# Clustered attention and a multiplicative feed-forward on one core: routing two heads ahead, engine copies for heads 0 and 1, halved weight loads

## The chip, the cores and the metric

The kernel runs on one core of one Trainium2 chip. The metric is the time on the device in microseconds (us); a kernel's time is the median of several executions. Kernels are compared only within the same rounds.

## The reference, cut to what matters

Each of 4 x 8 = 32 heads (768 tokens of width 64) is attention in which a query sees only the keys that fall into the same one of 16 clusters. The result, 3072 tokens of width 512, goes through a feed-forward network (FFN).

```python
q_assign = argmax(einsum('bhsd,hcd->bhsc', q_n, c_n), -1)      # c_n: normalised centroids of the head
k_assign = argmax(einsum('bhsd,hcd->bhsc', k_n, c_n), -1)
scores = where(q_assign[..., :, None] == k_assign[..., None, :], q @ k^T / 8, -1e9)
attn_out = softmax(scores) @ v
# ... (rearranged to x: [3072, 512])
out = ((x @ w1) * (x @ w2)) @ w3 @ w_out
```

## The kernel before: the parts that matter

The program is a row of periods. Period p computes the scores and exponentials of head p and the attention products of head p-1, prepares later heads, and fills TensorE's gaps with FFN work. Until period 8 this fill is the product w3 @ w_out ("fold": 8 items of transposes pt, then 16 items of products pw); the FFN proper (pu, then po) follows from period 9. Items are sorted by a number between 0 and 1, their place within the period, and every engine runs its own instructions in that order.

A head goes through these steps: three loads (q, k, v); POOL splits q and k into a bfloat16 part and its rest (stg); stg is turned into xqk, by TensorE for the first ten heads and by a DMA transpose for the others; TensorE multiplies xqk by the centroids (route, into prr); VectorE reduces that to one-hot rows (rsc, mx, oh); TensorE turns these (route_turn, into pso); VectorE scales them (ohT); four small DMAs put them below the head's q and k in xqk. There they work as a mask: equal clusters cancel an offset of -256 in the scores.

```python
def prep(g):
    ...                                          # cut
    eng = nc.vector if g < 1 else nc.gpsimd
    for lo, hi in ((0, NCH), (NCH, NC2)) if g < 1 else ((0, NC2),):
        eng.tensor_copy(out=stg[:, lo:hi, 0:D], in_=qk32[:, lo:hi])
        eng.tensor_tensor(out=stg[:, lo:hi, D:P], in0=qk32[:, lo:hi],
                          in1=stg[:, lo:hi, 0:D], op=ALU.subtract)
    nc.gpsimd.tensor_copy(out=vb[:, :, 0:D], in_=x32[:, 2])

def turn_dma(g):                                 # heads 10 and later
    st["xqk"] = xtp.tile([P, NC2, P], BF16, name="xqk")
    nc.sync.dma_start_transpose(out=st["xqk"], in_=st.pop("stg"))

# route_turn(g), its end:
    nc.vector.tensor_scalar(out=ohT, in0=pso, scalar1=msc[:, 0:1], scalar2=msc[:, 1:2],
                            op0=ALU.mult, op1=ALU.add)
    for a in range(4):
        nc.sync.dma_start(xqk[D : D + C, 3 * a : 3 * a + 3, :], ohT[32 * a : 32 * a + C])

def in_period(p):                                # p from -3
    for g in LOADS.get(p, []): load(g)
    if PE_HEADS <= p + 3 < NG: turn_dma(p + 3)
    ...                                          # prep of head p+3 (p+4 from head 10 on), one or two weight loads
    work += [((i + 0.5) / 9, it) for i, it in enumerate(score_items(p))]
    work += [(0.50, turn_pe(p + 2, 0)), (0.62, turn_pe(p + 2, 1))]      # below head 10
    work += [(0.02, route(p + 1)), (0.36, route_turn(p + 1))]
    work += [(0.23 + 0.13 * i, it) for i, it in enumerate(av_items(p - 1))]
    ...                                          # join at 0.93, fold or FFN items
```

A head's one-hot rows are asked for at 0.36 of the period before it is scored, 0.7 of a period before its first score.

The softmax here doesn't subtract the row's maximum and nothing guards it: scores larger than these inputs give would overflow.

## Time and profile before

| Kernel before | |
|---|---|
| time, median of 4 runs | 326.12 us (323.71 to 327.62) |
| span of the profiled run, which was a slow one (330.3 us) | 328.5 us |
| TensorE busy | 284.7 us, 87% |
| first score matmul, first exponential | 26.5 us, 27.1 us |
| TensorE's waits for one-hot rows | 14.6 us |

Engines are PE (TensorE; PEld is its weight load), DVE (VectorE), ACT (ScalarE), POOL and SP. L with a number is a line of the kernel; the changed kernel has other numbers for the same statements. The first view is the page of the kernel before: span, busy time per engine, and three rows of tenths over 40 equal slices of the span (TensorE busy, TensorE's granted clock, DMA engines busy).

```profile
span 328.5 us, 7415 instructions
...
PE 284.7 (87%) x2896; PEld 176.2 (54%) x2938; DVE 164.1 (50%) x340; ACT 195.4 (59%) x351; POOL 99.8 (30%) x110
...
PE   0357799699878999997899998999999999899995
...
PEclk9995699879997999997999999999999999999999
DMA  6973969922466586776765557655532012001103
```

TensorE is the busiest engine. It is idle for more than half of the first four slices (33 us), and its clock row has dips. The next view is who waited for whom on TensorE: us in total, number of waits, the longest.

```profile
engine line waited for: us in total, times, longest us
PE sc L341 <- DMA xqk<-ohT: 14.6, 8, 4.0
...
PE prr L293 <- DVE xT_all L406: 4.4, 8, 0.8
```

The scores wait for the one-hot rows eight times, 14.6 us together. Next, the table by stretches of the kernel before: bounds and length in us, then busy time with the number of instructions per engine, granted clock, DMA share and GB/s.

```profile
core 0: us, PE busy (x) PEld busy (x) DVE busy (x) ACT busy (x) POOL busy (x), PEclk, DMA share, GB/s
28.00:32.00 4.00, 4.00 (x31) 3.17 (x30) 2.21 (x4) 1.97 (x5) 3.56 (x4) 0.51 0.08 12
36.00:40.00 4.00, 4.00 (x42) 3.17 (x40) 1.17 (x2) 1.68 (x3) 0.21 (x1) 0.50 0.95 232
160.00:180.00 20.00, 19.77 (x221) 12.29 (x224) 11.16 (x25) 15.44 (x29) 6.36 (x7) 1.00 0.76 156
```

From 160 to 180 us TensorE is busy for 19.77 of 20 us at full clock; only less work for TensorE would help there. The two early stretches lie just behind a wait of 4.0 and 2.0 us: TensorE is busy throughout, but at half its clock. Busy time times (1 - clock), summed over stretches of 4 us, is 11.8 us in this profile. Last, the start in the timeline of the kernel before: start in us, duration, engine, line, what it does; in brackets the idle time of the engine and what ended it.

```profile
12.00 0.17 DVE L158 COPY cnsrc<-cnsrc 128x64 bf16<-128x64 bf16 x1
12.07 1.63 POOL L265 TENSOR_TENSOR stg<-x_196,stg 128x768 bf16<-128x768 f32 x1
12.11 1.63 DVE L157 COPY cnsrc<-cnsrc 128x64 bf16<-128x64 bf16 x1
...
20.60 2.49 SPq L324 DMA_DIRECT2D xqk<-ohT  x4
...
26.50 1.03 PE L341 MATMUL sc<-xqk 80*128 80x512 bf16 x2 [3.96 <-DMA xqk<-ohT]
...
27.14 1.09 ACT L345 ACTIVATE ex<-sc 128x512 bf16<-128x512 f32 x2 [20.90 <-PE sc L341]
```

The same copy of 64 columns takes 0.17 us, and 1.63 us when POOL's subtraction runs beside it. This is what the Trainium skill, "SBUF — State Buffer" (Who interferes with whom), describes: VectorE and POOL hold a port pair in turn, and the second one blocks. The rows of head 0 are sent at 20.6 us and the first score starts at 26.5 us. The waits of score matmuls for the rows are therefore one cost, the low clock behind them a second, and the long start a third.

### The profile page before, as it was taken

How to read it: one execution, taken by the hardware profiler on the slowest of the kernel's cores; microseconds unless marked ns; L12 is line 12 of the kernel's file. 1: busy time of each engine (PE TensorE's matmuls, PEld its weight loads, DVE VectorE, ACT ScalarE, POOL GpSimd, SP SyncE). 2: the span in 40 equal slices, each digit the busy share in tenths (PEclk: the TensorE clock that was granted, in tenths of full speed). 3: DMA queues.
4: the chain of work that ended last, by engine and by line, in shares of the span. 5: the costliest groups of instructions: out<-in, count | busy, mean ns of one | idle time of the engine just before them, and what ended most of it. 6: DMA issues, size and time to landing. Idle time of an engine off the chain costs nothing.

```text
span 328.5 us, 7415 instructions
## 1 busy us (share of the span) xinstructions
PE 284.7 (87%) x2896; PEld 176.2 (54%) x2938; DVE 164.1 (50%) x340; ACT 195.4 (59%) x351; POOL 99.8 (30%) x110
## 2 busy tenths in 40 slices
PE   0357799699878999997899998999999999899995
PEld 0245566366655566654566564656565655444442
DVE  8883456347663555544546444545454543332431
ACT  3004466447685987875687776787777777332330
POOL 3745138334355543433343233333300000000000
PEclk9995699879997999997999999999999999999999
DMA  6973969922466586776765557655532012001103
GB/s 221 198 128 97 190 133 245 243 72 85 117 155 132 142 165 155 144 189 190 140 146 126 129 168 185 155 127 128 150 87 57 8 38 89 17 0 70 59 2 128
DMA packets 59283, 41.16 MB, mean 125 GB/s; under 512 B 38768, under 2 KB 54128, under 8 KB 59248
## 3 DMA queue, kind: packets, MB, share of 16 engines
q1 hardware_dynamic: 56016, 35.44, 42.0%
q0 software_dynamic: 3232, 5.24, 9.6%
q8 instruction: 23, 0.38, 0.5%
q14 instruction: 12, 0.10, 0.1%
HBM read 29.39 MB, written 6.29 MB: 109 GB/s over the span
## 4 chain that ended last, share of the span: by engine, by line
PE 77%; DMA 11%; DVE 5%; ACT 4%; issue 1%; SPq 0%; POOL 0%; DVEq 0%
PE pu L216 24%; PE sc L341 13%; PE po L235 12%; PE av L373 11%; DMA xqk<-ohT 9%; PE sc L351 5%; PE pw L191 3%; DMA w3b<-in_moe_w_dram 2%; PE prr L293 2%; PE pso L316 2%; ACT ex L345 2%; PE pst L283 2%; PE psx L405 1%; PE pt L178 1%; DVE xT_all L406 1%
## 5 line engine op out<-in xcount | busy, mean ns | idle before, releaser
L345 ACT ACTIVATE ex<-sc 128x512 bf16<-128x512 f32 x192 | 110.6, 599 | 61.2 <-PE sc L341 60.8
L341 PE MATMUL sc<-xqk 80*128 80x512 bf16 x192 | 70.5, 397 | 15.5 <-DMA xqk<-ohT 14.6
L355 ACT ACTIVATE ex<-sc 128x512 bf16<-128x512 f32 x96 | 57.7, 601 | 23.3 <-PE sc L351 23.2
L373 PEld LDWEIGHTS <-ex 128*128 128x128 bf16 x1152 | 49.6, 101 | 13.2 <-issue 2.2
L224 DVE TENSOR_TENSOR ab<-pu,asb 128x512 bf16<-128x512 f32 x48 | 33.2, 691 | 43.2 <-PE pu L216 38.5
L216 PE MATMUL pu<-xT_all,w1b 128*128 128x512 bf16 x177 | 47.7, 383 | 1.1 <-issue 0.2
L216 PE MATMUL pu<-xT_all,w2b 128*128 128x512 bf16 x182 | 47.3, 378 | 0.5
L235 PE MATMUL po<-wc,ab 128*128 128x512 bf16 x183 | 45.8, 382 | 0.5
L222 ACT CAST asb<-pu 128x512 bf16<-128x512 f32 x48 | 28.2, 587 | 27.9 <-PE pu L216 27.9
L351 PE MATMUL sc<-xqk 80*128 80x256 bf16 x192 | 38.3, 281 | 0.1
L320 DVE TENSOR_SCALAR ohT<-pso,msc 128x384 bf16<-128x384 bf16 x32 | 15.2, 474 | 27.8 <-PE pso L316 25.0
L235 PEld LDWEIGHTS <-ab 128*128 128x128 bf16 x192 | 18.6, 97 | 18.5 <-issue 0.2
L216 PEld LDWEIGHTS <-w1b 128*128 128x128 bf16 x192 | 18.6, 98 | 18.3 <-issue 0.6
L216 PEld LDWEIGHTS <-w2b 128*128 128x128 bf16 x192 | 18.4, 97 | 18.2 <-issue 0.3
L341 PEld LDWEIGHTS <-xqk 80*128 80x128 bf16 x192 | 17.3, 99 | 20.1 <-DMA xqk<-ohT 16.1
L351 PEld LDWEIGHTS <-xqk 80*128 80x128 bf16 x192 | 17.5, 101 | 15.4 <-issue 2.8
L297 DVE TENSOR_REDUCE rsc<-prr 128x192 f32<-128x384 f32 x32 | 17.7, 554 | 15.8 <-PE prr L293 15.8
L293 PEld LDWEIGHTS <-xqk 128*128 128x128 bf16 x384 | 14.3, 96 | 9.5 <-issue 5.8
L243 DVE COPY osb<-po 128x512 f32<-128x512 f32 x12 | 8.3, 692 | 21.0 <-PE po L235 19.0
L293 PE MATMUL prr<-cnt_181,xqk 128*128 128x32 bf16 x384 | 14.8, 177 | 4.6 <-DVE xT_all L406 4.4
L386 DVE TENSOR_TENSOR xtm<-av,rcp 128x384 bf16<-128x384 f32 x32 | 17.8, 557 | 1.1
L191 PE MATMUL pw<-wob,w3T 128*128 128x512 bf16 x56 | 16.0, 401 | 0.4
(170 smaller groups left out, 316.8 us busy)
## 6 DMA issues: line engine op xcount, KB each, us to landing
out_dram<-osb SPq DMA_DIRECT2D x24, 256.0 KB, 2.0
w3b<-in_moe_w_dram POOLq DMA_DIRECT2D x4, 512.0 KB, 7.7
xqk<-ohT SPq DMA_DIRECT2D x128, 12.0 KB, 1.8
wob<-in_moe_w_out_dram POOLq DMA_DIRECT2D x2, 512.0 KB, 7.0
w1b<-in_moe_w_dram POOLq DMA_DIRECT2D x2, 512.0 KB, 7.2
w2b<-in_moe_w_dram POOLq DMA_DIRECT2D x2, 512.0 KB, 10.0
xqk<-stg SPq DMA_TRANSPOSE x22, 4.5
x_105<-in_q_dram SPq DMA_DIRECT2D x1, 192.0 KB, 2.4
```

Of the source, the lines that this page charges most:

```text
L191: nc.tensor.matmul(st[jc], lhsT=w3T[:, kc, jc * P : (jc + 1) * P], rhs=wob[:, kc], start=(kc == 0), stop=(kc == 7),)
L216: nc.tensor.matmul(pu, lhsT=wb[:, fc, jc * P : (jc + 1) * P], rhs=xT_all[:, fc, t0 : t0 + TB], start=(fc == 0), stop=(fc == 3),)
L222: nc.scalar.copy(out=st["a"], in_=pu)
L224: nc.vector.tensor_tensor(out=st["ab"][:, jc], in0=pu, in1=st.pop("a"), op=ALU.mult)
L235: nc.tensor.matmul(st["o"], lhsT=st["ab"][:, jc, sub * P : (sub + 1) * P], rhs=wc[:, jc], start=(jc == 0), stop=(jc == 7),)
L293: nc.tensor.matmul(prr[:, j], lhsT=st["xqk"][:, j, :], rhs=cnt2[:, g % H], start=True, stop=True)
L341: nc.tensor.matmul(sc, lhsT=xqk[0:KR, NCH + 2 * pr + part, :], rhs=xqk[0:KR, 0:4, :], start=True, stop=True,)
L345: nc.scalar.activation(out=ex[:, part, 0:512], in_=sc, func=ACT.Exp, scale=SM_SCALE)
L351: nc.tensor.matmul(sc[:, i], lhsT=xqk[0:KR, NCH + 2 * pr + i, :], rhs=xqk[0:KR, 4:6, :], start=True, stop=True,)
L355: nc.scalar.activation(out=ex[:, :, 512:S], in_=sc, func=ACT.Exp, scale=SM_SCALE)
L373: nc.tensor.matmul(st["av"][:, sub, 0:VCOL], lhsT=st["exs"][j // 2][:, j % 2, sub * P : (sub + 1) * P], rhs=st["vb"][:, j, 0:VCOL], start= ...
L386: nc.vector.tensor_tensor(out=xtm_cur[0][:, :, (h % 2) * D : (h % 2) * D + D], in0=av[:, :, 0:D], in1=rcp.unsqueeze(2).to_broadcast([P, NC ...
```

## The change

Its intent: route two heads ahead, so that the one-hot rows are in place early; take POOL out of the way of the first two heads; place their rows by engine copies and not by DMA; load the weights in 20 pieces and not 10, two a period. The core of the diff, with cuts marked and some lines joined:

```diff
+FIRST = 2
+DIRECT = 2
+    for i in range(8):
+        wloads.append((w3b[:, i], w3v[:, i]))      # 20 loads in place of 10; w_out, w1, w2 alike (cut)
 def prep(g):
+        if g < FIRST:                                # per half, q or k; v on POOL as before (cut)
+                    nc.scalar.copy(out=stg[:, half, 0:D], in_=x32[:, i])
+                    nc.vector.tensor_tensor(out=stg[:, half, D:P], in0=x32[:, i],
+                                            in1=stg[:, half, 0:D], op=ALU.subtract)
 # route_turn(g)
+            if g < DIRECT:
+                for a in (2, 0, 3, 1):
+                    dst, src = xqk[D : D + C, 3 * a : 3 * a + 3, :], pso[32 * a : 32 * a + C]
+                    if a < 2: nc.scalar.copy(out=dst, in_=src)
+                    else:     nc.vector.tensor_scalar(out=dst, in0=src, scalar1=MASKB,
+                                                      scalar2=-MASKB, op0=ALU.mult, op1=ALU.add)
+                return
 # in_period(p)
-            work += [(0.50, turn_pe(p + 2, 0)), (0.62, turn_pe(p + 2, 1))]
-            work += [(0.02, route(p + 1)), (0.36, route_turn(p + 1))]
+            work += [(0.03, turn_pe(p + 2, 0)), (0.13, turn_pe(p + 2, 1))]
+        if p == 0: work += [(0.02, route_turn(1))]
+            work += [(0.33, route(p + 2)), (0.67, route_turn(p + 2))]
-        wload()                                      # one a period, two from period 2
+        wload(); wload()
```

Periods -3 to -1 become one hand-ordered stretch, begin(): loads of head 0 on two queues, centroid norm, heads 0 and 1 prepared and turned, route(0), route_turn(0), route(1), with head 2's preparation among them. The fold items are spread anew (1, 2, 2, 2, 1, 1, then 5 a period). The centroid chain has fewer small operations.

## The prediction

> **What bounds the kernel now.** TensorE: 284.7 of 328.5 us busy (busy table, 87%), against ACT 59%, DVE 50%; from 160 to 280 us the busy-by-stretch table has it at 97%. Three losses:
>
> 1. The start. The timeline has the first score matmul at 26.5 us. VectorE's centroid chain takes 5.95 to 13.74 us: most ops take 0.15 us, but four take 0.96 to 1.63 us while POOL prepares head 1. The Trainium skill, "SBUF — State Buffer" (Who interferes with whom), says a VectorE op with two SBUF inputs or in a 2-port mode blocks against a GpSimd op; the trace agrees (the same 64-column copy: 0.17 and 1.63 us).
> 2. Waits of scores for one-hot rows (xqk<-ohT): 14.6 us of TensorE in the table of waits, 4.0 of them at the start; 8.8% of the chain. Routing products wait 4.4 us more for the xT_all copy.
> 3. The clock: 0.51 at 28-32 us, 0.50 at 36-40 and 64-68, 0.57 at 100-104, 0.65 at 152-156, each after a wait of 2 to 4 us. "TensorE: Matmul & The Clock Gate" (Part 1) says an idle window of about 3.4 us halves it; the trace roughly agrees. Busy time times (1 - clock) sums to about 11 us.
>
> **What the change does.** TensorE work stays about 273 us at full clock (busy times clock, summed).
>
> - Start: head 0's q and k land near 4 us on two queues; ScalarE casts, VectorE subtracts, POOL keeps away. I estimate the centroid chain ends near 10 us, first routing product near 12, head 1's one-hots (serial: one PSUM buffer) near 17.5, first score 18.5, first exponential 20 (behind a 1.28 us table load) instead of 27.1. About 8 us earlier, but four fold transposes that filled this time (3.5 us) come later: net 5.
> - One-hots are issued over a period (6 to 8 us) ahead; issue to landing is 1.8 us in the median, 6.1 at worst. The other 10.6 us of waits nearly vanish, with about 8 of 11 us of clock loss. Routing at 0.33 instead of behind the join saves about 3 of 4.4 us.
> - Weight loads: same bytes, twice the issues (about 0.75 us of POOL each), spread to period 8. The first 85 us must now carry about 66 us of DMA that had 100. I estimate 4 us of new waits.
>
> **Critical path.** All lies there up to the pure FFN tail at 283 us. The first FFN product (period 9) should start near 83 to 88 us instead of 101.
>
> Sum: 325.9 - 5 - 10 - 8 - 3 + 4 = 304; I say 305 for imperfect packing.
>
> **Predicted: 305 us**, 8 in 10 between 297 and 313. Faster by over 2%: 0.96; within 2%: 0.03; slower: 0.01.
>
> **What shows it right.** First score at 17 to 20 us, first exponential near 20; TensorE's waits for xqk<-ohT under 2 us; clock near 1.0 after about 25 us (mean 0.98 or more); first pu matmul before 90 us; TensorE at 92% or more; still 45 us from last exponential to end.
>
> **What would make it wrong.** Periods 0 to 8 bound by DMA or POOL (pst waiting for stg, fold transposes for w3b); VectorE's routing chain ending after TensorE wants the one-hot transpose, a third of a period later; ScalarE holding the start, as head 1's row copies stand ahead of the first exponential; a clock left low by the sparse first 20 us.

## More of the kernel before

Executions of one kernel spread by up to three per cent here. One that took over 1.5% more than the fastest of its kernel is called slow; medians count all executions, ratios the fast ones alone.

A DMA transpose asked for at the start of period p is read by the routing product at 0.02 of period p+2: a lead of 2.02 periods.

## The result, and the profile after

| | before | after |
|---|---|---|
| time, median of 4 runs | 326.12 us | 313.62 us (313.19 to 315.29) |
| ratio | | 0.963 (95% interval 0.956 to 0.970) |
| span of the profiled run | 328.5 us | 313.4 us |
| first score, first exponential | 26.5, 27.1 us | 19.5, 22.2 us |
| TensorE's waits for one-hot rows (xqk<-ohT) | 14.6 us | none in the table |
| TensorE's waits for DMA transposes (xqk<-stg) | none | 8.8 us |
| busy time times (1 - clock), by the clock record | 11.8 us | 2.6 us |
| first FFN product (pu) | 101.8 us | 90.6 us |

A ratio is the mean time of one kernel's fast runs over that of the kernel before's fast runs of the same rounds, so it is not quite the ratio of the medians. The kernel is 3.7% faster. The prediction was 305 us with a range to 313 us: right in direction, too low in size, by 8.6 us.

The page of the changed kernel, in the same rows:

```profile
span 313.4 us, 7404 instructions
...
PE 279.5 (89%) x2899; PEld 170.9 (55%) x2938; DVE 156.4 (50%) x335; ACT 201.9 (64%) x363; POOL 101.4 (32%) x118
...
PE   1459997997599899979999999999999998999995
...
PEclk9999999999799999999999999999999999899999
DMA  6865569989916966587666686656732011002003
```

TensorE is mostly busy in slices 4 to 10 and its clock record is nearly whole, but slice 11 (78 to 86 us) is half empty. Up to about 27 us the record can't be trusted: it reads 1.00, while matmuls take the time of half a clock (last section). The waits of TensorE in the changed kernel (us in total, times, longest):

```profile
PE prr L317 <- DMA xqk<-stg: 8.8, 5, 5.5
...
PE pso L340 <- DVE oh_114 L325: 2.9, 2, 1.4
PE pso L340 <- DVE oh_113 L325: 1.9, 2, 1.0
...
PE pst L303 <- POOL stg L286: 0.5, 1, 0.5
```

The rows are no longer waited for. In their place stand routing products that wait for a DMA transpose. The table by stretches of the changed kernel, columns as before, around the largest of these waits (the DMA share is summed from the times of packets and can pass 1):

```profile
76.00:80.00 4.00, 0.73 (x15) 0.45 (x13) 0.64 (x1) 1.19 (x2) 0.00 (x0) 1.00 1.10 102
80.00:84.00 4.00, 1.81 (x16) 0.91 (x17) 1.20 (x3) 0.00 (x0) 0.00 (x0) 0.72 1.19 229
84.00:88.00 4.00, 3.94 (x40) 2.46 (x40) 1.90 (x5) 2.06 (x4) 2.92 (x3) 0.85 0.48 109
```

TensorE works 0.73 us of the 4 from 76 to 80, and the idle time is followed by a clock of 0.72 and 0.85. "TensorE: Matmul & The Clock Gate" (Part 1) says about 3.4 us of idleness are enough; the trace agrees with this wait of 5.46 us, and the clock record shows no other loss before 264 us. It is not the least that is enough: in the kernel before, low clock also came behind single waits of 2.04 us (36 us), 1.84 us (150 us) and 0.94 us (100 us). The timeline of the changed kernel there, SPq being the queue on SP that issues DMAs:

```profile
68.33 5.74 SPq L294 DMA_TRANSPOSE xqk<-stg  x1
...
82.19 0.50 PE L317 MATMUL prr<-cnt_110,xqk 128*128 128x32 bf16 x12 [5.46 <-DMA xqk<-stg]
```

The first DMA transpose (head 10) is asked for at 68.33 us. Its issue alone holds the queue for 5.74 us; the other 21 transposes of this profile took 1.3 to 2.3 us there. The routing product that reads it starts at 82.19 us. The list of DMA issues between 68 and 70 us (size in KB, us from issue to landing):

```profile
w2b<-in_moe_w_dram POOLq DMA_DIRECT2D x1, 256.0 KB, 8.4
w1b<-in_moe_w_dram POOLq DMA_DIRECT2D x1, 256.0 KB, 11.1
...
xqk<-stg SPq DMA_TRANSPOSE x1, 13.8
```

The transpose lands after 13.8 us, while two weight loads around it take 8.4 and 11.1 us. The median of all 22 transposes of this profile is 4.5 us. The start in the timeline of the changed kernel:

```profile
9.62 0.34 PE L317 MATMUL prr<-cnt_110,xqk 128*128 128x32 bf16 x6 [0.52 <-ACT xqk L306]
...
10.01 2.43 DVE L279 TENSOR_TENSOR stg<-x_129,stg 128x384 bf16<-128x384 f32 x2 [1.38 <-ACT stg L278]
...
12.11 1.82 POOL L286 TENSOR_TENSOR stg<-x_152,stg 128x768 bf16<-128x768 f32 x1
12.36 0.55 DVE L321 TENSOR_REDUCE rsc<-prr 128x192 f32<-128x384 f32 x1
...
14.75 0.35 DVE L350 TENSOR_SCALAR xqk<-pso 16x384 bf16<-16x384 bf16 x1 [0.60 <-PE pso L340]
...
15.20 0.47 ACT L348 COPY xqk<-pso 16x384 bf16<-16x384 bf16 x1 [1.04 <-DVE xqk L350]
...
16.09 0.47 ACT L348 COPY xqk<-pso 16x384 bf16<-16x384 bf16 x1 [0.43 <-DVE xqk L350]
...
19.46 0.63 PE L377 MATMUL sc<-xqk 80*128 80x512 bf16 x1
...
20.89 1.28 ACT L381 ACT_TABLE_LOAD   x1
...
22.19 1.08 ACT L381 ACTIVATE ex<-sc 128x512 bf16<-128x512 f32 x2
...
27.79 0.38 PE L377 MATMUL sc<-xqk 80*128 80x512 bf16 x1
```

Three things stand here. Head 0's routing product ends near 10 us, but VectorE's reduction of it (L321) starts only at 12.36 us, because two subtractions for head 1, at 0.55 us each when alone, take 2.43 us beside POOL. The row copies of head 0 follow one another, VectorE, ScalarE, VectorE, ScalarE, 14.75 to 16.56 us. And the table load of the exponential (1.28 us) stands behind the copies of head 1; that these would stand ahead of the first exponential is a risk that the prediction named. Besides, a score matmul of 512 columns takes 0.63 us at 19.46 and 0.38 us at 27.79.

### The profile page after: what moved, and what is told of

Same layout as the page of the kernel before. It is cut to its first block, busy times and chain, and to the rows that moved or that the text cites. A ratio compares the mean times of both kernels' runs of the same rounds, so it can differ in the third digit from the quotient of the medians.

```text
span 313.4 us, 7404 instructions
## 1 busy us (share of the span) xinstructions
PE 279.5 (89%) x2899; PEld 170.9 (55%) x2938; DVE 156.4 (50%) x335; ACT 201.9 (64%) x363; POOL 101.4 (32%) x118
## 3 DMA queue, kind: packets, MB, share of 16 engines
q0 software_dynamic: 3392, 5.24, 11.8%
## 4 chain that ended last, share of the span: by engine, by line
PE 69%; DMA 15%; DVE 5%; SPq 3%; ACT 3%; issue 2%; POOL 1%; POOLq 0%; DVEq 0%; ACTq 0%
PE pu L225 23%; DMA xqk<-stg 12%; PE po L244 12%; PE sc L377 10%; PE av L409 8%; PE sc L387 5%; PE pw L200 3%; SPq L79 3%; PE prr L317 3%; DMA x_543<-in_k_dram 2%; PE pso L340 2%; PE pst L303 2%; PE psx L441 2%; ACT ex L381 1%; DVE rsc L321 1%
## 5 line engine op out<-in xcount | busy, mean ns | idle before, releaser
L377 PE MATMUL sc<-xqk 80*128 80x512 bf16 x192 | 71.8, 388 | 1.8 <-ACT ex L381 1.1
L409 PEld LDWEIGHTS <-ex 128*128 128x128 bf16 x1152 | 47.5, 98 | 15.8 <-issue 0.8
L244 PE MATMUL po<-wc,ab 128*128 128x512 bf16 x182 | 44.8, 378 | 0.5
L321 DVE TENSOR_REDUCE rsc<-prr 128x192 f32<-128x384 f32 x32 | 17.8, 557 | 40.7 <-PE prr L317 40.7
L387 PE MATMUL sc<-xqk 80*128 80x256 bf16 x192 | 37.4, 276 | 0.1
L387 PEld LDWEIGHTS <-xqk 80*128 80x128 bf16 x192 | 16.8, 99 | 13.8 <-issue 2.2
L317 PEld LDWEIGHTS <-xqk 128*128 128x128 bf16 x384 | 13.8, 97 | 14.7 <-DMA xqk<-stg 11.1
L356 DVE TENSOR_SCALAR ohT<-pso,msc 128x384 bf16<-128x384 bf16 x30 | 14.2, 473 | 8.9 <-PE pso L340 8.2
L303 PE MATMUL pst<-ident,stg 128*128 128x128 bf16 x120 | 12.2, 250 | 7.1 <-DVE stg L279 6.7
```

Source lines behind the costliest of these rows:

```text
L244: nc.tensor.matmul(st["o"], lhsT=st["ab"][:, jc, sub * P : (sub + 1) * P], rhs=wc[:, jc], start=(jc == 0), stop=(jc == 7),)
L303: nc.tensor.transpose(out=pst[:, j], in_=st["stg"][:, half * NCH + j], identity=ident)
L317: nc.tensor.matmul(prr[:, j], lhsT=st["xqk"][:, j, :], rhs=cnt2[:, g % H], start=True, stop=True)
L321: nc.vector.tensor_reduce(out=rsc, in_=prr, axis=AX.X, op=ALU.add)
L377: nc.tensor.matmul(sc, lhsT=xqk[0:KR, NCH + 2 * pr + part, :], rhs=xqk[0:KR, 0:4, :], start=True, stop=True,)
L387: nc.tensor.matmul(sc[:, i], lhsT=xqk[0:KR, NCH + 2 * pr + i, :], rhs=xqk[0:KR, 4:6, :], start=True, stop=True,)
```

## The experiments

Each run was timed beside the kernel before. Runs of one group shared a chip. The expectation is quoted. Kernels of one group are compared by their fast runs. Group 1 has no run of the changed kernel itself.

| Group | Kernel | median us | mean of the fast runs, us (their number) | ratio to before (95%) |
|---|---|---|---|---|
| 1 | w_early | 307.65 | 305.0 (2) | 0.940 (0.927 to 0.952) |
| 1 | pe12 | 309.01 | 309.3 (4) | 0.953 (0.943 to 0.963) |
| 1 | lead | 303.11 | 302.4 (3) | 0.931 (0.918 to 0.945) |
| 1 | start | 307.69 | 307.0 (3) | 0.946 (0.936 to 0.956) |
| 2 | after_again | 309.76 | 308.2 (4) | 0.948 (0.941 to 0.956) |
| 2 | route1 | 321.20 | 320.7 (3) | 0.992 (0.984 to 1.000) |
| 2 | nodirect | 310.16 | 308.7 (4) | 0.950 (0.943 to 0.956) |
| 2 | best | 304.47 | 304.2 (4) | 0.936 (0.929 to 0.942) |
| 3 | after_3 | 311.27 | 309.1 (4) | 0.947 (0.940 to 0.955) |
| 3 | lead_2 | 306.40 | 306.1 (5) | 0.938 (0.933 to 0.943) |
| 3 | lead_nd | 306.06 | 305.6 (4) | 0.936 (0.931 to 0.942) |
| 3 | bigw | 311.31 | 310.3 (5) | 0.951 (0.944 to 0.957) |
| 4 | after_4 | 310.51 | 310.1 (4) | 0.950 (0.943 to 0.957) |
| 4 | early0 | 303.15 | 302.1 (4) | 0.926 (0.919 to 0.932) |
| 4 | lead_late | 308.61 | 308.1 (5) | 0.944 (0.939 to 0.949) |
| 5 | lead_3 | 304.66 | 304.5 (5) | 0.939 (0.934 to 0.945) |
| 5 | early0_2 | 302.20 | 302.2 (6) | 0.932 (0.928 to 0.936) |
| 5 | early0_few (wrong) | 299.35 | 299.3 (6) | 0.924 (0.919 to 0.928) |

Theory A was: the weight loads, which now reach period 8, collide with the first DMA transposes. The rival B: the transposes are asked for too late. turn_dma stayed at the start of period p, but its reader moved from 0.02 of period p+2 to 0.33 of period p+1, so the lead shrank from 2.02 to 1.33 periods.

### w_early: weight loads over sooner

```diff
-        wload()
-        wload()
+        wload(); wload(); wload()
```

> The changed kernel with three weight loads a period instead of two, so that they are all issued by period 5 and not period 8; nothing else. Theory A (the weight loads that now reach period 8 collide with the first DMA transposes and that costs the missing time): the first transpose lands in under 6 us instead of 13.8 us, the 5.5 us wait of TensorE for xqk<-stg at 77 to 82 us goes, and the time falls by 5 to 6 us, to about 308 us; the waits of 1 to 2 us after 90 us stay. Rival B (the transposes are only asked for too late, 1.33 periods before their use): the long wait mostly stays, time within 2 us of 313.6.

The first transpose landed in 4.4 us in place of 13.8 us (7.7 to 11.6 us in the three repeats below), and the first wait went: A holds for it. The profile is of a slow run, but the next one, of a fast run, shows the same landing. But TensorE still waited 4.0 us for transposes, only later. From the timeline of w_early, its longest wait:

```profile
134.37 0.46 PE L317 MATMUL prr<-cnt,xqk 128*128 128x32 bf16 x12 [2.43 <-DMA xqk<-stg]
```

There are no weight loads at 134 us; B holds for this one. The median lies 6 us below the one of the changed kernel, but only 2 to 4 us below its medians of the other groups, and the ratios (0.940 here, 0.947 to 0.950 there) are not apart: what A costs in time is not shown.

### pe12: two more heads turned by TensorE

```diff
-PE_HEADS = 10
+PE_HEADS = 12
```

> The changed kernel with heads 10 and 11 also turned by TensorE, so that the first DMA transpose comes two periods later, after the last weight load. Theory A: the first transpose lands in under 6 us, the 5.5 us wait goes; TensorE pays about 1 us more for each of the two heads; net 3 to 4 us faster, about 310 us. Rival B: a first transpose is always late by this schedule, the wait of about 5 us moves two periods later, time 313 to 316 us.

The first transpose, now at 86.4 us and behind the weights, landed in 4.4 us, so no long first wait came back: A again. The waits of B stayed (3.2 us, the longest 1.7 us). The expected 310 us came (309.0), but the ratio, 0.953, is no better than that of the changed kernel in the other groups (0.947 to 0.950): no gain in time is shown.

### lead: every transpose a period sooner

```diff
-        if PE_HEADS <= p + 3 < NG:
-            turn_dma(p + 3)
+        if PE_HEADS <= p + 4 < NG:
+            turn_dma(p + 4)
-            ahead = 3 if g < PE_HEADS else 4
+            ahead = 3 if g < PE_HEADS else 5
```

(Loads one period sooner from head 10 on; stg 4 buffers, xqk 7, vb 8, so that no buffer is taken early. One condition on the preparation is cut.)

> The changed kernel with each DMA transpose (and the preparation before it) asked for one period earlier, 2.33 periods before the routing product that reads it, weight loads as they are. Rival B: all waits for xqk<-stg go (8.8 us on TensorE), also those of 1 to 2 us after 90 us: 9 us faster, about 305 us. Theory A alone: the first transpose still takes over 10 us to land, in the same weight traffic, but the longer lead may hide it; then only the 5.5 us are won, about 308 us. If both hold, 304 to 306 us.

No wait for a transpose is left in the table of waits. The page of this kernel:

```profile
span 300.7 us, 7403 instructions
...
PE 276.2 (92%) x2899; PEld 170.8 (57%) x2938; DVE 157.8 (52%) x337; ACT 202.0 (67%) x363; POOL 101.6 (34%) x118
...
PE   1559988899999999999999999999999997999994
...
PEclk9999999999999999999999999999999999999999
```

The transposes did not become faster everywhere. One line of the view of the tile xqk in this kernel, the time from issue to landing of all transfers into it:

```profile
DMA to landing us min/median/max: 1.7/2.7/9.9
```

The worst is still 9.9 us; the lead hides it. The remedy for B alone removes the waits of both A and B. The added buffers were not tried alone. In the profile on record the first transpose went out at 68.33 us, 0.1 us behind the loads ahead of it on its queue, so no missing buffer held it there.

### after_again, after_3, after_4: the changed kernel repeated

> The changed kernel unaltered, on the chip of the next three, since the timed runs of one kernel spread by over 1%. Expected 311 to 315 us. Under theory A the landing of the first DMA transpose varies from run to run with the traffic, so a spread of 2 to 5 us is expected, and a wait for xqk<-stg of 2 to 6 us before the first transposed head.

> The changed kernel unaltered, again, as the yardstick for the next three on one chip. Expected 307 to 314 us, with a wait for xqk<-stg before head 10 whose length (1.6 and 5.5 us in two profiles) changes from run to run.

> The changed kernel unaltered, as the yardstick of this call. Expected 307 to 314 us.

The medians were 309.8, 311.3 and 310.5 us, against 313.6 us; the first lies below the 311 to 315 us that I expected, and its wait, 1.6 us, below the 2 us. The four profiles show how much hangs on the transposes:

| Profile of the changed kernel | first transpose landed in | waits for xqk<-stg, total | the wait before head 10 | span |
|---|---|---|---|---|
| on record | 13.8 us | 8.8 us | 5.5 us | 313.4 us |
| after_again | 9.3 us | 3.9 us | 1.6 us | 304.7 us |
| after_3 (slow) | 11.6 us | 7.0 us | 3.8 us | 313.8 us |
| after_4 | 7.7 us | 5.4 us | 0.9 us | 307.9 us |

The line of after_again's timeline, to set beside the one above:

```profile
77.80 0.47 PE L317 MATMUL prr<-cnt,xqk 128*128 128x32 bf16 x12 [1.59 <-DMA xqk<-stg]
```

Spans run with the waits in these four, after_3 with a start 2 us later besides. So the landing under traffic can be a large part of the spread of this kernel; runs without a profile do not show it.

### lead_2: the longer lead beside the changed kernel

> The longer lead of the DMA transposes alone, against the changed kernel on the same chip. If the waits for transposes, which the prediction did not have, are its main miss: 6 to 9 us below the changed kernel (about 302 to 304 us) and a smaller spread of the times. If the two differ by under 3 us, the difference seen before was the chip's, and the miss lies elsewhere.

Between fast runs it lay 3.0 us below the changed kernel of its group (4.9 us between the medians, which hold slow runs). That is half of the expected 6 to 9 and only just at the 3 us below which I would have given the difference to the chip. The smaller spread did not come either (304.7 to 312.8 us, beside 306.9 to 315.7 us). The intervals of the two ratios overlap by a hair (0.940 to 0.943). Over all groups, the mean of the ratios is 0.949 for three repeats of the changed kernel and 0.936 for three of the longer lead: 0.012 of about 326 us, or 4 us. That is less than the 3.9 to 8.8 us of waits that went. One reason shows in the profiles: lead_2 and lead_3 waited 2.3 and 3.2 us for one-hot rows again, which lead did not.

### route1: routing one head ahead again

```diff
-        work += [(0.03, turn_pe(p + 2, 0)), (0.13, turn_pe(p + 2, 1))]
-        work += [(0.33, route(p + 2)), (0.67, route_turn(p + 2))]
+        work += [(0.50, turn_pe(p + 2, 0)), (0.62, turn_pe(p + 2, 1))]
+        work += [(0.02, route(p + 1)), (0.36, route_turn(p + 1))]
```

(Cut: route(1) leaves begin(), and route_turn(1) its place in period 0.)

> The changed kernel with routing one head ahead again (products at 0.02 and one-hot transposes at 0.36 of the period before use, head turns at 0.50 and 0.62), all the rest of the change kept. If the lead of the routing is what removed the waits for one-hot rows and the clock loss, TensorE waits 6 to 10 us for xqk<-ohT again, the clock falls to 0.5 behind several of these waits, the waits for xqk<-stg vanish (the DMA transposes then have two periods), and the time is 318 to 322 us. If the gain came from the start alone, time stays near 313 us.

The time was 321.2 us, 12.5 us above the changed kernel of its group between fast runs, and most of the gain was gone. Two lines of route1's table of waits on TensorE:

```profile
PE sc L377 <- DMA xqk<-ohT: 11.6, 7, 2.5
...
PE prr L317 <- DVE xT_all L442: 3.9, 6, 0.8
```

The waits of the kernel before are back (14.6 us there), and 5.0 us of clock loss with them, although the first exponential came at 17.4 us. A start 10 us sooner than before brought 0.8% (interval 0 to 1.6%): by far the most of the gain is the lead of the one-hot rows. This run has no waits for transposes; its lead for them is again two periods.

### nodirect and lead_nd: rows of heads 0 and 1 by DMA

```diff
-DIRECT = 2
+DIRECT = 0
```

> The changed kernel with the one-hot rows of heads 0 and 1 sent by DMA as for all other heads. If placing them by engine copies carries the earlier start, first scores of head 0 come no later (its rows have 2 us more of routing of head 1 to land in) but those of head 1 do not wait either, as a period lies between: then the engine copies are worth 0 to 1 us. If a DMA of the rows lands in 4 to 6 us in the busy start, as in the kernel before, the first score moves from 19.5 to 20 to 22 us and the time rises by 1 to 3 us.

The first exponential came sooner, at 18.6 us, not later: nothing alternates between two engines, and the first exponential no longer stands behind ScalarE's copies of head 1. The time did not follow (308.7 us beside 308.2 between fast runs). The line of nodirect's timeline at the first transpose:

```profile
76.56 0.51 PE L317 MATMUL prr<-cnt,xqk 128*128 128x32 bf16 x12 [3.79 <-DMA xqk<-stg]
```

Against 1.59 us in after_again of the same group, 2.2 us of the 3.4 us won at the start were given back here.

> Longer lead, and the rows of heads 0 and 1 by DMA. In the changed kernel the DMA rows brought the first exponential from 22.0 to 18.6 us and yet no time, while the wait for the first transpose grew from 1.6 to 3.8 us. Theory D (time won at the start is given back at the first DMA transpose, which lands at a time set by the DMA traffic and not by TensorE): with the longer lead the 3 us come through, 299 to 301 us. Rival: periods 0 to 8 have another bound (VectorE's one-hots, POOL) that eats the 3 us: same time as the longer lead alone, within 1 us.

This did not settle it: in the profile of lead_nd, that of a slow run, the rows of head 0 were late, the first score waited 3.0 us for them, and the first exponential came at 22.96 us. Rows by DMA came in time for head 0 in one of these two profiles and not in the other. The time equalled that of lead_2.

### bigw: the old size of weight load

```diff
-    for i in range(8):
-        wloads.append((w3b[:, i], w3v[:, i]))
+    for i in range(4):
+        wloads.append((w3b[:, 2 * i : 2 * i + 2], w3v[:, 2 * i : 2 * i + 2]))
     # w_out, w1, w2 alike; one load a period in place of two
```

> The changed kernel with the weights in 10 loads of 512 KB as before, one a period in place of two halves (all issued by period 7 or 8, as in the changed kernel). If the size of a load matters (a large load standing ahead of the x loads and transposes), the waits for xqk<-stg grow and the time rises by 2 us or more. If only the bytes matter, time is within 1 us of the changed kernel; POOL then spends 10 times 0.75 us less.

The medians are equal (311.3 us); between fast runs the old size is 1.1 us slower, with overlapping ratios (0.951 and 0.947). The smaller loads are worth nothing that these runs can tell from noise. The edit also takes one load out of begin(): in its profile head 1's subtractions took 1.15 us and the first exponential came at 20.8 us.

### start: the row copies on one engine, the table loaded early

```diff
-                        nc.scalar.copy(out=dst, in_=src)
+                        nc.vector.tensor_copy(out=dst, in_=src)
         turn_pe(0, 0)()
+        nc.scalar.activation(out=tiny, in_=cst["ss"], func=ACT.Exp, scale=SM_SCALE)   # one column
```

> The changed kernel with the one-hot rows of heads 0 and 1 all copied by VectorE (no hand-over between the two engines) and the table of the exponential loaded earlier by a one-column exponential behind the first copy of head 0. Theory C (the start is 2 us later than forecast because the four copies of a head alternate ScalarE and VectorE one after the other, 1.85 us a head, with the table load after them): copies 1.45 us a head, first exponential near 20 us instead of 22.2, time 1 to 2 us lower, about 312 us. If the start is limited by something else, the first exponential moves by under 0.5 us.

The first exponential moved by 0.4 us only, from 22.2 to 21.8 us. The copies took 1.46 us a head, as expected, but the chain ahead of them was later in this run, and the two subtractions of head 1 took 3.04 us beside POOL. Theory C's own part did come: from first score to first exponential it took 0.67 us in place of 2.73. But the first score, which stands behind the routing of head 1, came at 21.14 in place of 19.46 us. As an account of the late start, theory C is at most a part. The better time (307.7 us) cannot be put down to the start; the wait for the first transpose happened to be 2.4 us here.

### best: everything at once

It joins lead, w_early and start, and puts two weight-load issues on POOL ahead of head 2's preparation.

> Longer lead of the DMA transposes, three weight loads a period, the rows of heads 0 and 1 by VectorE alone with the exponential's table loaded early, and two weight-load issues put on POOL before it prepares head 2, so that head 1's subtractions on VectorE are over before POOL's copy begins. Waits for xqk<-stg 0; the two subtractions of head 1 take about 1.2 us in place of 2.4 to 3.0; first exponential at 20 to 21 us; clock 1.0; time 299 to 302 us, 1 to 3 us below the longer lead alone (303.1 us).

A miss in time: 304.5 us in place of 299 to 302. The two subtractions took 1.93 us (1.2 expected), the first exponential came at 20.6 us, and the time was that of the longer lead (ratio 0.936). TensorE now waited 7.1 us for the one-hots of VectorE (oh), where lead had 4.3 us. I have not separated which of the parts raised it.

### lead_late: the one-hot transposes later

```diff
-            work += [(0.33, route(p + 2)), (0.67, route_turn(p + 2))]
+            work += [(0.33, route(p + 2)), (0.82, route_turn(p + 2))]
```

> Longer lead, and the one-hot transposes at 0.82 of the period in place of 0.67, so that VectorE's chain has half a period and not a third. TensorE's waits for oh (3.9 us in 6 waits in the profile of the longer lead, about 2 us of them after the start) fall by 1 to 2 us, unless the shorter way from the one-hots to the scores brings back waits for xqk<-ohT. Time 0 to 2 us lower, ratio 0.932 to 0.938.

A miss: 308.6 us, ratio 0.944, no better than the longer lead (0.931 to 0.939). The waits for oh fell from 3.9 to 2.7 us, but a new one came up in the table of waits:

```profile
PE psx L441 <- DVE ohT L356: 3.9, 9, 1.1
```

pso and the join's psx share the one buffer of psum_r; brought close together, they wait for each other.

### early0 and early0_2: head 1 routed inside period 0

```diff
-        route(1)()                                   # end of begin()
-        if p == 0:
-            work += [(0.02, route_turn(1))]
-        if p + 2 < NG:
+        if p == 0:
+            work += [(0.15, route(1)), (0.42, route_turn(1)), (0.60, route(2)), (0.90, route_turn(2))]
+        elif p + 2 < NG:
```

(on lead, with the two edits of start)

> Longer lead of the DMA transposes, and head 1's routing moved from before the first scores into period 0 (product at 0.15, one-hot transpose at 0.42, head 2's at 0.60 and 0.90), rows of heads 0 and 1 by VectorE, exponential's table loaded early. In the run with routing one head ahead the first exponential came at 17.4 us in place of 22.0; it should come at 17 to 18 us here. If the start is worth its time (the forecast's 2 us of late start are then part of the miss): 3 to 4 us below the longer lead, a ratio near 0.927 of the kernel before. If theory D holds (periods 0 to 8 have another bound, DMA traffic or VectorE with POOL), first pu product still at 84 to 85 us and the ratio near 0.938.

> The kernel of early0 again, now beside the longer lead on one chip. If the earlier start comes through: 2.5 to 4 us below it. If it is lost in periods 0 to 8, as its first pu product (83.6 us beside 84.0 to 84.7 us) suggests: less than 1.5 us below it.

Its yardstick on the same chip, the longer lead once more:

> The longer lead alone, as the yardstick of the next two on one chip. Expected 303 to 307 us, ratio 0.93 to 0.94.

The first exponential came at 16.6 and 16.0 us. Early0's ratio was 0.926, as expected for a start that comes through. Beside the longer lead on one chip the time was 302.2 against 304.5 us between fast runs: 2.3 us for a start 6.3 us sooner (22.4 to 16.0 us). That is just short of what I had set for "comes through" (2.5 us), and above what I had set for "lost" (1.5 us). The first FFN product moved only from 83.0 to 82.2 us, so most of the time won at the start is lost before period 9. Early0_2 has the lowest median of the correct kernels, and its six runs lay within 3 us (300.8 to 303.8).

### early0_few: most of the weight traffic taken away

```diff
-# 20 weight loads
+# 4 weight loads; the other chunks of w3, w_out, w1 and w2 are read from these four
```

> Wrong result on purpose: the kernel of early0 with 4 weight loads in place of 20 (the other chunks of the weights are read from these four), TensorE's work the same; 4.2 MB less over the DMA and 16 loads less to issue on POOL, all in periods 0 to 8. If the weight traffic is what eats the earlier start (theory D), the waits for xqk<-ohT and for the head preparation in periods 4 to 8 go, the first pu product moves from 83.6 to 80 to 81.5 us and the time falls by 2 to 4 us. If not, the first pu product stays within 1 us and so does the time.

Its output is wrong, which doesn't matter for the time. The table by stretches, 20 to 85 us, first of early0_2, then of early0_few:

```profile
20.00:85.00 65.00, 61.50 (x821) 43.45 (x822) 43.50 (x91) 45.48 (x83) 38.12 (x46) 1.00 0.95 183
```

```profile
20.00:85.00 65.00, 63.44 (x840) 44.45 (x839) 45.53 (x97) 47.47 (x87) 32.02 (x34) 1.00 0.51 132
```

The DMA share falls from 0.95 to 0.51, TensorE gains 1.9 us of work in the stretch, its waits for rows and for preparation go from the table, the first FFN product moves to 79.6 us, and the time is 2.8 us lower between fast runs; the intervals of the ratios just touch (0.928), but all six runs lie below all six of early0_2. Weight traffic, together with its issue on POOL, is where a part of an early start is lost. The run does not tell the DMA from POOL, which was busy 6.1 us less.

## Why the prediction was wrong

**What held.** TensorE bounds the kernel, and from 160 to 260 us it is busy for 98.96 of 100 us in the changed kernel. The waits for one-hot rows went to nothing (10.7 us after the start, 10 forecast). The wait behind the join, 4.4 us, went whole where I had counted 3. The clock loss fell from 11.8 to 2.6 us by the record; counting the half clock up to 26.9 us that the record leaves out, the gain behind the first exponential is some 7 us (8 forecast). "Faster", given a chance of 0.96, came.

**The step that failed** is the term "I estimate 4 us of new waits". I looked for them in loads and in POOL's preparation, and I said that TensorE might wait for oh. I missed that routing at 0.33 of a sooner period takes two thirds of a period from the lead of the DMA transposes, which the diff leaves where they were. Measured in the profile: 8.8 us for transposes, and after the start 2.4 us for one-hots (0.4 us before) and 0.5 us for stg, some 11 us in place of 4. (In the three repeats the waits for transposes were 3.9 to 7.0 us.) It was in view: the diff moves a reader and leaves the request. "DMA: Bandwidth & Descriptors" (Rules for kernel authors) says to issue a DMA early and wait on it late; the runs agree (8.8 us of waits with a lead of 1.33 periods, none with 2.33). With the lead restored these waits are zero and the time falls by 3.0 us in one group (about 4 us over all), to medians of 303 to 306 us, which is the predicted time. Two causes make the waits: the weight traffic that now reaches period 8 (w_early and pe12 remove the first wait), and the lead itself (the later waits stay in both).

**The base of the sum** was a second fault. The losses were read from a slow run's profile (330.3 us), but taken from the fast runs' 325.9 us: 4.4 us too low. From its own base the same sum gives 308 us. That the longer lead lands on the predicted 305 us is therefore partly luck: between the profile of lead (302.5 us) and that of the kernel before 27.8 us went, where the sum had 22, and that made up for the wrong base.

**The start** came out near its forecast, "about 8 us earlier, net 5", but also by luck. The first exponential came at 22.2 us and not at 20, 4.9 us sooner than before. The copies of head 1 and the table load stood ahead of it, and head 1's subtractions beside POOL held head 0's reduction for 2.4 us. Against that, the four fold transposes that moved behind it cost almost nothing net. The transposes and the routing of head 2 and more scores took their place: up to the first exponential TensorE had done some 4.2 us of work at full clock before and 4.0 us after (estimates from the counts of matmuls and their spacing later in the profiles). With the lead restored, a start 6.3 us sooner was worth 2.3 us.

**The sum, corrected**, from the two profiles, in us:

| Term | forecast | measured |
|---|---|---|
| start | -5 | -4.7 |
| waits for one-hot rows after the start | -10 | -10.7 |
| clock behind the first exponential | -8 | -6.9 |
| routing behind the join | -3 | -4.4 |
| new waits | +4 | +11.3 |
| sum | -22 | -15.4 |

The spans differ by 15.1 us. The start and the clock hold estimates: 0.2 us for the work above, and 2.0 us for 4.07 us of busy time at half clock from 22.2 to 26.9 us that the record does not show.

**What stays open.** The four runs of the changed kernel lay 2 to 4 us above its medians in three other groups, where the forecast's range to 313 us would have held. The varying landing of the first transpose can make such a difference, but runs without a profile do not show it. How much of the changed kernel's clock gain fast runs keep is not known, as the profile of the kernel before is of a slow run. Nor is it settled whether weight traffic costs early0 its time through DMA or through POOL.

## What to carry to other kernels

When a reader of a transfer is moved to an earlier place, look at every request that feeds it: what counts is the distance from request to reader, against the landing time under traffic and not its median (here 13.8 us against 4.5). A long wait on the busiest engine can cost more than itself, since the clock falls behind it (here 5.5 us of wait, and 1.1 us of clock from 80 to 88 us); a request made a period sooner took such waits away at the price of a few buffers. Losses read from a profile are to be taken from the time of that same run. And time won at a start counts only as far as the stages behind it are not short of something else.

## What the Trainium skill lacked or had wrong

- "DMA: Bandwidth & Descriptors" (DMA Transpose): it gives no time for a transpose under traffic. Here a DMA transpose of a [128, 12, 128] bfloat16 tile landed in 4.5 us in the median, in 13.8 us amid weight loads, and its issue held SP's queue for 5.74 us then.
- "TensorE: Matmul & The Clock Gate" (Part 1): it says that the array starts at half clock, and the trace agrees (first score matmuls 0.63 us, 0.38 us later; two in a row 1.07 and 0.60 us, so that the second adds 0.44 and 0.22). It warns that a trace's clock events can be unreliable, but not that the record can read 1.00 in that stage: the changed kernel's record shows 1.00 up to 80 us, although the matmuls of 512 columns took 0.63 us up to 26 us. The first low clock must be read from durations.
- "ScalarE: Activation LUTs" (What ACT_TABLE_LOAD costs): it gives 2.66 us for a switch of table sets, 1.28 us of load and 1.38 us of drain. Here the load took 1.28 us and the exponential started 0.02 us behind it, with the instruction before the load ending 0.01 us ahead of it.
- "SBUF — State Buffer" (Who interferes with whom): the trace agrees with the rule. What the page has no number for is a whole chain: two subtractions of 0.55 us took 1.15 to 3.09 us in different runs, and one one-hot comparison of 0.36 us took up to 1.8 us beside POOL.
